# Cutting every 24th matmul of the w_out product into two column parts

## The chip, the cores and the metric

The kernel runs on one core of one Trainium2 chip. The metric is device time of one execution in microseconds (us); lower is better. Three runs of the kernel before took 463.36, 464.67 and 464.75 us, so its median is 464.67 us.

## The reference

The program is a chain of three layers with no normalisation between them, all in float32:

```python
# q, k, v: (2, 12, 448, 64)
scores = q @ k.T / sqrt(64), masked above the diagonal
x = softmax(scores) @ v                      # 2 x 448 tokens, 768 wide
g = relu(x @ w_in) ** 2                      # w_in (768, 2048)
y = g @ w_out                                # w_out (2048, 768): the product that is changed
h = max(y @ w1, y @ w2, y @ w3)              # w1..w3 (768, 768)
out = h @ w_o                                # (768, 768)
```

## The kernel before

Activations lie transposed, features on the 128 partitions and tokens along the columns, so that a block of 128 x 128 weights is the stationary operand of a matmul and the 448 tokens of one batch entry are its moving operand. A matmul of this kind is one instruction that loads the weights and one that streams the 448 columns into a bank of PSUM.

The dense layers are computed in a split form. Every value is cut into a high part that the float32r format holds and a remainder (`hi_lo`, L119), and a product is three passes (`PASSES`, L477): high by high, high by low, low by high. All matmuls of the dense layers are float32r; scores, transposes and the product with v are plain float32.

The products with w_in and with w1 to w3 (`Sevens.run`, L496) use seven block products in place of eight, as Strassen's scheme has it. They run from L499, 448 columns each, nine matmuls to a slot. The last product (`product`, L749, and the loop at L1009) has 384 columns to a matmul.

The w_out product is plain. It is made by `out_slots` (L610), which is called for the six blocks m of 128 output features. For each, the 16 blocks f of the inner dimension come in slots of two or three f; for each f, the three passes; for each pass, the two batch entries b, which share their weights and have a bank of PSUM each. That is 6 x 16 x 3 x 2 = 576 matmuls, all from L627. A slot's weights (`Quarter`, L181) are made by one cast on ScalarE and one subtraction on VectorE three slots ahead. At the end of a block m, ScalarE copies the two banks out (L644).

The order of the work is written out by hand. The attention's steps follow the list `ORDER`; after them the loop at L997 goes through the slots, issues the slot's matmuls, and then what stands `beside` it on the other engines. The first two blocks of the w_out product are interleaved with the last two slots of the w_in product. The matmuls of TensorE run in the order in which they are issued.

Of the kernel before, what the change touches and what calls it, by code (L numbers as in the profile page):

```python
# [18 lines left out]
MASKED = -1.0e30  # L19
WARM = 10  # L20
PR = 2
NORM = ((4, 7), (2, 4), (0, 2))
LEAD = 3
RING = 5
# [40 lines left out]
def tile_attention_moe_moe(  # L65
# [23 lines left out]
    nc = tc.nc  # L89
    B, NP, P, S = k.shape  # L90
# [8 lines left out]
    KFF = DFF // P  # L99
# [95 lines left out]
    def decoded(w):  # L195
        return Op(w.join, [Op(w.cast)], w)
# [98 lines left out]
    def constants(pool):  # L295
        ident = shared["ident"] = pool.tile([P, P], F32, name="ident", bufs=1)
        make_identity(nc, ident)
        for m, parts in ((NQ * P, 1), (S, 2)):
            n = P // parts
            mask = pool.tile([P, m], F32, name=f"mask{parts}", bufs=1)  # L300
            nc.gpsimd.memset(mask, 0.0)
            for j in range(parts):
                r = slice(j * n, (j + 1) * n)
                nc.gpsimd.affine_select(
                    out=mask[r, m - n:], in_=mask[r, m - n:], compare_op=ALU.is_ge, fill=MASKED,
                    base=0, pattern=[[-1, n]], channel_multiplier=1,
                )
            masks.append(mask)
# [5 lines left out]
    start = [kc * S - kc * (kc - 1) // 2 * P for kc in range(NK)] + [S * NK - NK * (NK - 1) // 2 * P]  # L314
# [6 lines left out]
    class Pair:  # L321
# [30 lines left out]
        def least(self, u):  # L352
            if not hasattr(self, "st"):
                self.pr = prs[self.i % PR]
                self.st = att.tile([P, 3, 2 * NQ + 1], F32, tag="st", name="st")
# [92 lines left out]
        def steps(self):  # L448
# [4 lines left out]
            for c in range(len(keys)):  # L453
# [5 lines left out]
                e[f"n{c}'"] = lambda c=c: self.norm(nc.vector, c)  # L459
            for n, c in enumerate(NORM):  # L460
                e[f"r{n}"] = lambda c=c: self.recip(*c)
# [145 lines left out]
    ]  # L607
    gh, gl, y = {}, {}, {}

    def out_slots(m):  # L610

        acc = [ps[i][:, :S] for i in ((6, 7), (0, 1), (2, 3), (4, 5), (6, 7), (0, 1))[m]]
        res = []
        for k0 in range(0, KFF, KDM):
            nk = min(KDM, KFF - k0)
            w = Weight(w_out, k0, nk, m * P, P, 2)
            d, h = decoded(w), -(-nk // 2)
            for r0, r1 in ((0, h), (h, nk)):
                quarter = Quarter(
                    [d], lambda w=w, r0=r0, r1=r1: w.t[:, r0:r1], lambda w=w: w.kept, r1 - r0  # L620
                )

                def run(quarter=quarter, k0=k0 + r0, k1=k0 + r1):
                    for f in range(k0, k1):
                        for e, (ew, ex) in enumerate(PASSES):
                            for b in range(B):
                                nc.tensor.matmul(  # L627
                                    acc[b], quarter.t[:, ew, f - k0], (gh, gl)[ex][f][0][:, b],
                                    start=f == 0 and e == 0, stop=f == KFF - 1 and e == 2,
                                    skip_group_check=True,  # L630
                                )
                    if m == KDM - 1:
                        for f in range(k0, k1):
                            units.give(gh[f][1])
                            units.give(gl[f][1])

                res.append(Slot(run, quarter, None, (m, k0 + r0)))

        def evac():
            if m == KDM - 1:  # L640
                shared["y"] = acc
                return [], []
            y[m] = units.take(f"y{m}", F32)
            return [lambda b=b: nc.scalar.copy(y[m][0][:, b], acc[b]) for b in range(B)], []  # L644

        res[-1].evac = evac
        return res
# [8 lines left out]
    ]  # L656
    head, tail = pipelined(firsts)
    outs = [out_slots(m) for m in range(KDM)]
    slots = head + [outs[0][0], tail[0], outs[0][1], tail[1], *outs[0][2:]]
    for e in outs[1:]:  # L660
# [157 lines left out]
    at = dict(load=0)  # L818
# [137 lines left out]
    with tc.tile_pool(name="att", bufs=2) as att:  # L956
        constants(att)
        prs = [att.tile([P, offs[-1]], F32, name=f"pr{n}", bufs=1) for n in range(PR)]
        warm = att.tile([P, 2 * P], FR, name="warm", bufs=1)
# [11 lines left out]
        for n in range(BESIDE):  # L971
            x, nm = slots[n].name
# [36 lines left out]
    for f in range(KF2):  # L1009
        x = zr["t"][0][:, f] if f < KH else None  # L1010
        x = [x[:, 0], x[:, 1]] if f < KH else [e[0][:, last] for e in z2[f]]
        for e, (ex, ew) in enumerate(((0, 0), (0, 1), (1, 0))):
            for acc, cs in zip(rest, (left, right)):
                nc.tensor.matmul(  # L1014
                    acc, x[ex], wo[f][ew][0][:, cs], start=f == 0 and e == 0,
                    stop=f == KF2 - 1 and e == 2, skip_group_check=True,
# [110 lines left out]
```

## Time and profile before

| | before |
|---|---|
| median of three runs | 464.67 us |
| profiled execution, its own time | 468.29 us |
| its span, first to last instruction | 466.5 us |
| outside the span | 1.8 us |
| granted TensorE clock, mean | 1.000 |
| matmuls and weight loads | 2434 each |
| matmuls of L627 | 576 |

Rows come from one profiled execution, whose time is 3.6 us above the median of the runs without a profile. PE is TensorE streaming columns, PEld TensorE loading weights; the two overlap. DVE is VectorE, ACT ScalarE, POOL GpSimd. Matmuls are pipelined, and the duration that a row gives for one of them is modelled and longer than its distance to the next, so distances are read from the chain of waits, which lists merged stretches with their start, their length and the count of instructions.

### The profile page before, as it was taken

What the parts mean: (1) busy time and instruction counts of PE and PEld (TensorE: products, weight loads), DVE (VectorE), ACT (ScalarE), POOL (GpSimd) and SP (SyncE); (2) the same over time, 40 slices, a digit from 0 to 9 for tenths busy, and PEclk for the clock granted to TensorE, in tenths of its full rate; (3) what the DMA queues carried; (4) which work ended last, traced back from release to release, by engine and by line L of the source; (5) the groups of instructions that cost most, each with busy time, mean ns of one, the idle gap of its engine ahead of it and who ended that gap; (6) DMA issues with size and microseconds to landing.
All of it is one profiled execution on the core that took longest, in us unless ns stands there. A gap on an engine that the chain in (4) does not pass through costs nothing.

```text
span 466.5 us, 6969 instructions
## 1 busy us (share of the span) xinstructions
PE 460.7 (99%) x2434; PEld 402.0 (86%) x2434; DVE 364.3 (78%) x813; ACT 283.1 (61%) x609; POOL 42.4 (9%) x90
## 2 busy tenths in 40 slices
PE   8999999999999999999999999999999999999997
PEld 5766676899999999899999999999999999999996
DVE  5999999998888899992322272898888988898963
ACT  5999999756555557952323254566457656665541
POOL 3656455000000000000000000000000000000000
PEclk9999999999999999999999999999999999999999
DMA  6463543223344441435323423342256466400014
GB/s 214 138 219 127 173 161 91 69 73 112 96 127 136 137 135 45 136 108 186 98 84 112 136 74 111 131 135 68 91 182 197 147 199 203 136 1 1 34 52 152
DMA packets 47619, 56.28 MB, mean 121 GB/s; under 512 B 1761, under 2 KB 43873, under 8 KB 47585
## 3 DMA queue, kind: packets, MB, share of 16 engines
q1 hardware_dynamic: 47296, 55.61, 37.0%
q8 instruction: 19, 0.31, 0.3%
q10 hardware_dynamic: 288, 0.23, 0.2%
q14 instruction: 16, 0.12, 0.1%
HBM read 53.08 MB, written 2.75 MB: 120 GB/s over the span
## 4 chain that ended last, share of the span: by engine, by line
PE 96%; DVE 3%; issue 0%; DVEq 0%
PE ps L499 47%; PE ps L627 26%; PE ps L752 7%; PE ps L347 7%; PE ps L386 4%; PE ps L417 4%; PE ps L1014 1%; PE ps L962 1%; DVE pr L358 1%; DVE s L124 0%; DVE pr L378 0%; DVE a L117 0%; DVE wd L169 0%; DVE st L374 0%; DVE wq L117 0%
## 5 line engine op out<-in xcount | busy, mean ns | idle before, releaser
L499 PE MATMUL ps<-s,wq 128*128 128x448 f32 x612 | 129.6, 368 | 0.0
L499 PEld LDWEIGHTS ps<-s,wq 128*128 128x128 f32 x612 | 114.8, 188 | 11.7 <-ACT s L509 0.2
L499 PE MATMUL ps<-a,wq 128*128 128x448 f32 x459 | 100.0, 370 | 0.0
L627 PE MATMUL ps<-gh,wq 128*128 128x448 f32 x384 | 95.3, 368 | 0.0
L499 PEld LDWEIGHTS ps<-a,wq 128*128 128x128 f32 x459 | 85.5, 188 | 9.0 <-issue 0.4
L117 DVE TENSOR_TENSOR wq<-wd,wq 128x384 fp32r<-128x384 f32 (+1 forms) x87 | 46.0, 533 | 49.3 <-ACT wq L114 45.0
L627 PEld LDWEIGHTS ps<-gh,wq 128*128 128x128 f32 x384 | 72.1, 188 | 7.3
L114 ACT CAST wq<-wd 128x384 fp32r<-128x384 f32 (+1 forms) x87 | 42.9, 499 | 53.8 <-PE ps L627 33.1
L164 ACT CAST up<-wr 128x768 f16<-128x768 bf16 (+1 forms) x58 | 60.8, 1049 | 7.1 <-DMA wr<-in_moe_w 2.1
L169 DVE SCALAR_TENSOR_TENSOR wd<-wr,up 128x768 int32<-128x768 int32 (+1 forms) x58 | 53.8, 928 | 6.1 <-ACT up L164 5.4
L627 PE MATMUL ps<-gl,wq 128*128 128x448 f32 x192 | 55.2, 368 | 0.0
L509 ACT COPY s<-ps 128x448 f32<-128x448 f32 x51 | 27.1, 533 | 37.6 <-PE ps L499 37.1
L366 ACT ACTIVATE pr<-pr,st 128x384 f32<-128x384 f32 (+3 forms) x84 | 44.1, 529 | 5.4 <-DVE st L358 5.2
L117 DVE TENSOR_TENSOR wq<-wt,wq 128x384 fp32r<-128x384 f32 x68 | 37.2, 551 | 9.4 <-ACT wq L114 9.1
L114 ACT CAST wq<-wt 128x384 fp32r<-128x384 f32 x68 | 34.3, 515 | 16.5 <-DVE wt L124 13.4
L378 POOL TENSOR_SCALAR pr<-pr,st 128x256 f32<-128x256 f32 (+3 forms) x77 | 39.9, 534 | 37.6 <-DVE st L374 22.7
L627 PEld LDWEIGHTS ps<-gl,wq 128*128 128x128 f32 x192 | 36.0, 188 | 3.6
L358 DVE CUSTOM_DVE_ANT_0 pr<-ps,mask 128x384 f32<-128x384 f32 (+3 forms) x84 | 34.5, 443 | 5.5 <-PE ps L347 4.9
L347 PE MATMUL ps<-k,q 64*128 64x128 f32 (+3 forms) x168 | 35.5, 445 | 0.0
L386 PEld LDWEIGHTS ps<-ident,pr 128*128 128x128 f32 x192 | 21.6, 140 | 7.5 <-issue 3.1
L386 PE MATMUL ps<-ident,pr 128*128 128x128 f32 x192 | 26.3, 276 | 0.3 <-DVE pr L378 0.3
L124 DVE TENSOR_TENSOR s<-ps,s 128x448 f32<-128x448 f32 (+1 forms) x31 | 18.2, 598 | 9.4 <-ACT s L509 4.5
(108 smaller groups left out, 494.0 us busy)
## 6 DMA issues: line engine op xcount, KB each, us to landing
wr<-in_moe_w_out SPq DMA_DIRECT2D x18, 768.0 KB, 4.3
wr<-in_moe_w SPq DMA_DIRECT2D x18, 768.0 KB, 4.3
wr<-in_moe_w_in SPq DMA_DIRECT2D x16, 768.0 KB, 4.7
v<-in_v SPq DMA_DIRECT2D x12, 256.0 KB, 4.6
wr<-in_moe_w_out SPq DMA_DIRECT2D x6, 512.0 KB, 3.5
q<-in_q SPq DMA_DIRECT2D x11, 256.0 KB, 2.7
out<-s SPq DMA_DIRECT2D x14, 192.0 KB, 1.9
k<-in_k SPq DMA_DIRECT2D x11, 224.0 KB, 2.9
```

What stands on the lines that cost most here:

```text
L114: nc.scalar.copy(hi, src)
L117: nc.vector.tensor_tensor(out=lo, in0=src, in1=hi.bitcast(F32), op=SUB)
L164: nc.scalar.copy(self.up.bitcast(FH)[:, :, 1::2], self.top)
L169: nc.vector.scalar_tensor_tensor(out=self.t.bitcast(I32), in0=self.rest, scalar=13, in1=self.up.bitcast(I32), op0=ALU.logical_shift_right, ...
L347: nc.tensor.matmul(sc[:, :keys[w]], self.n["q"][r, w // 2 * P:(w // 2 + 1) * P], self.n["k"][r, :keys[w]], start=True, stop=True,)
L358: nc.vector.tensor_tensor_reduce(out=self.pr[:, offs[u]:offs[u] + n], in0=self.sc[u][:, :n], in1=mask[:, mask.shape[1] - n:], scale=-SCALE ...
L366: nc.scalar.activation(sl, sl, ACTF.Exp, bias=self.st[:, 0, u:u + 1], scale=-1.0, accum_out=self.st[:, 1, u:u + 1],)
L378: engine.tensor_scalar(sl, sl, self.st[:, 2, u:u + 1], 1.0, op0=ALU.mult, op1=ALU.mult)
L386: nc.tensor.transpose(pt[:, i], self.pr[:, offs[u] + kc * P:offs[u] + (kc + 1) * P], shared["ident"])
L499: nc.tensor.matmul(self.acc[n], self.q[n].t[:, ew, i], X[OPERANDS[n]][i][:, ex], start=n in ("M1", "M2", "M5") and i == 0 and e == 0, stop ...
L627: nc.tensor.matmul(acc[b], quarter.t[:, ew, f - k0], (gh, gl)[ex][f][0][:, b], start=f == 0 and e == 0, stop=f == KFF - 1 and e == 2, skip ...
L752: nc.tensor.matmul(acc, a, b, start=start and i == 0 and e == 0, stop=i == KH - 1 and e == 2, skip_group_check=True,)
```

## The change

`matmul_in_parts` takes the place of the call at L627. It counts its calls; where the count leaves a remainder of 12 when divided by 24, it issues two matmuls with the same weights in place of one, the first over columns 0 to c and the second over columns c to 448 of the same bank. The cut c goes through a list of twelve places, so that each is used twice. The 576 calls give 24 such pairs: in each block m at f = 2, 6, 10 and 14, pass high by high, b = 0. No flag of these matmuls starts or ends an accumulation.

```diff
+EVERY = 24
+CUTS = (224, 256, 288, 320, 352, 384, 400, 416, 432, 440, 192, 128)
...
+    nth = [0]
+
+    def matmul_in_parts(acc, w, x, start, stop):
+
+        n, at = nth[0], [0, S]
+        nth[0] += 1
+        if n % EVERY == EVERY // 2:
+            at.insert(1, CUTS[n // EVERY % len(CUTS)])
+        for c0, c1 in zip(at, at[1:]):
+            nc.tensor.matmul(
+                acc[:, c0:c1], w, x[:, c0:c1], start=start, stop=stop, skip_group_check=True,
+            )
+
...
                             for b in range(B):
-                                nc.tensor.matmul(
+                                matmul_in_parts(
                                     acc[b], quarter.t[:, ew, f - k0], (gh, gl)[ex][f][0][:, b],
-                                    start=f == 0 and e == 0, stop=f == KFF - 1 and e == 2,
-                                    skip_group_check=True,
+                                    f == 0 and e == 0, f == KFF - 1 and e == 2,
                                 )
```

## Rows read from the trace of the kernel before

**Rows 1.** The page: span, busy time by engine, granted clock, chain by engine and line.
```profile
span 466.5 us, 6969 instructions
PE 460.7 (99%) x2434; PEld 402.0 (86%) x2434; DVE 364.3 (78%) x813; ACT 283.1 (61%) x609; POOL 42.4 (9%) x90
...
PEclk9999999999999999999999999999999999999999
...
PE 96%; DVE 3%; issue 0%; DVEq 0%
PE ps L499 47%; PE ps L627 26%; PE ps L752 7%; PE ps L347 7%; PE ps L386 4%; PE ps L417 4%; PE ps L1014 1%; PE ps L962 1%; DVE pr L358 1%; DVE s L124 0%; DVE pr L378 0%; DVE a L117 0%; DVE wd L169 0%; DVE st L374 0%; DVE wq L117 0%
```

**Rows 2.** Chain in order of time (start, us, what, count), the w_out stretch.
```profile
183.81 3.65 PE ps L627 x18
187.46 2.03 PE ps L499 x9
189.49 3.72 PE ps L627 x18
193.21 1.86 PE ps L499 x9
195.07 111.60 PE ps L627 x540
```

**Rows 3.** Chain in order of time, from the w_out stretch to the end.
```profile
306.67 113.46 PE ps L499 x549
...
428.53 6.24 PE ps L1014 x36
434.77 28.30 PE ps L752 x162
463.07 0.02 issue
463.09 0.56 DVE s L124
```

**Rows 4.** Waits of the weight loads from 187 us to the end.
```profile
PEld ps L499 <- ACT s L509: 0.3, 1, 0.3
PEld ps L752 <- issue: 0.2, 1, 0.2
```

**Rows 5.** Instructions in order of time, weight loads alone, after a pause of float32r work.
```profile
88.66 0.19 PEld L499 LDWEIGHTS ps<-a,wq 128*128 128x128 f32 x1
...
88.76 0.40 PEld L499 LDWEIGHTS ps<-a,wq 128*128 128x128 f32 x2
```

**Rows 6.** The same around the restart at 444 us.
```profile
444.06 0.19 PEld L752 LDWEIGHTS ps<-piece 128*128 128x128 f32 x1 [0.25 <-issue]
...
444.17 0.19 PEld L752 LDWEIGHTS ps<-piece 128*128 128x128 f32 x1
```

**Rows 7.** Chain in order of time, attention: transposes and plain float32 scores.
```profile
24.33 0.87 PE ps L386 x8
...
30.73 0.76 PE ps L347 x2
```

**Rows 8.** Groups by shape, matmuls: columns of the moving operand, count, busy us, mean ns.
```profile
L347 PE MATMUL ps<-k,q 128*128 128x448 f32 x24 | 10.9, 545 | 0.0
...
L962 PE MATMUL ps<-warm 128*128 128x256 f32 x10 | 2.5, 432 | 2.0 <-DVE warm L960 2.0
```

**Rows 9.** Groups by shape, weight loads of the w_out product.
```profile
L627 PEld LDWEIGHTS ps<-gh,wq 128*128 128x128 f32 x384 | 72.1, 188 | 7.3
...
L627 PEld LDWEIGHTS ps<-gl,wq 128*128 128x128 f32 x192 | 36.0, 188 | 3.6
```

**Rows 10.** Waits on the w_out matmuls, 183 to 307 us (total us, times, longest).
```profile
ACT wq L114 <- PE ps L627: 33.1, 13, 3.3
ACT y L644 <- PE ps L627: 14.2, 4, 3.6
```

## The prediction

> **What bounds the kernel now.** First the page. TensorE streams columns for 460.7 of 466.5 us, no other engine is above 78%, and the chain that ended last lies 96% on TensorE, 26% of the span on L627, the line that is changed [rows 1]. The granted clock stands at its full value, the 2.4 GHz level, in every slice, so the clock is not what is at stake.
>
> Next the chain in order of time, which gives the distance from one matmul to the next. In the w_out stretch one piece holds 540 matmuls of L627 in 111.60 us: 206.7 ns each, with nothing between them [rows 2]. So the stretch has no idle time into which an added instruction could go. The waits say the same from the other side: ScalarE waits 33.1 us and 14.2 us for these matmuls [rows 10], and TensorE waits for nobody there.
>
> Then what comes behind. From 306.67 us 549 matmuls of L499 take 113.46 us, again 206.7 ns each, and the last product runs to 463.07 us [rows 3]. The waits of the weight loads from 187 us on add up to 0.5 us in two places [rows 4]. A delay of TensorE in the w_out product is therefore not swallowed later, beyond at most that 0.5 us: the other engines only get more time to be ready. Nothing of the order on the other engines changes, no wait is added, and no buffer comes free earlier.
>
> The time of the change is thus the time that 24 pairs take on TensorE, less that of 24 whole matmuls, and nearly all of it shows at the end.
>
> **What a pair costs.** Each of the 24 removed matmuls gives back 206.7 ns [rows 2]. Each pair adds one instruction of weight loading, since in this kernel every matmul has a load of its own, also the two of b = 0 and b = 1 that share weights (2434 of each [rows 1]).
>
> The wide part first. The trace has float32r matmuls of two widths at full clock: 448 columns at 206.7 ns, and 384 columns at 6.24 us / 36 = 173.3 ns [rows 3]. That is 33.4 ns for 64 columns, 0.52 ns per column. I take this line for all wide parts: 440 columns 202.5 ns, 416 190, 400 181.7, 352 156.6, 320 139.9, 288 123.2, 256 106.5. With 0.417 ns per column (one column per cycle at 2.4 GHz) from the 384-column point down, 320 columns would be 146.6 and 256 120 ns.
>
> The narrow part next. The trace shows no float32r matmul at full clock under 384 columns, so its cost has to be bounded. From below: the weights of the matmul behind it have to be loaded while it streams. Where float32r work sets in after a pause, two loads start one right behind the other, at 88.66 and 88.76 us and again at 444.06 and 444.17 us [rows 5, 6]; at the rows' precision that is 0.10 to 0.11 us, and I take 108 ns. Transposes of 128 columns with one load each follow each other at 0.87 us / 8 = 109 ns [rows 7]. So a matmul cannot follow the last sooner than 108 ns, however narrow, unless the load is hidden by something else. In the stretch as it is, the 206.7 ns of the columns hide it; with a narrow part that cover is gone, and the load is what is late next. From above: the load's own recorded duration is 188 ns [rows 9], and the shortest distance seen between float32r matmuls without a pause is the 173.3 ns of 384 columns; if that already were the load's limit, every narrow part would cost 173.3 ns. (The ten matmuls of 256 columns at the program's start take 0.25 us each [rows 8], longer than those of 384 and 448 columns later. What holds them is peculiar to the start, so they set no end; with parts at 0.25 us the sum would be 24 x 293 ns = 7.0 us.) I take 108, because the two restarts show float32r loads at that distance themselves and no row shows a load that held up a matmul for longer.
>
> The sum, each pair as the larger of line and 108 ns for either part, less 206.7 ns, in the order of the cuts: 224, 256 and 192: 9.3 ns each (two times 108); 288: 24.5; 320 and 128: 41.2 each; 352: 57.9; 384: 74.6; 400: 82.9; 416: 91.3; 432: 99.7; 440: 103.8. Together 645 ns, and each cut comes twice: **1.29 us**. The line is not critical: with 0.417 ns per column under 448 instead, the sum is 1.36 us. With a floor of 110 ns it is 1.35 us. With a fixed 13.3 ns for every part on top of the load (a floor of 121) it is 1.70 us.
>
> Against the profiled execution: 468.29 + 1.3 = 469.6 us, with a span of 467.8. Against the median of the runs: 464.67 + 1.3 = **466.0 us**, 0.28% more.
>
> **What speaks against it.** The row shows 206.7 ns for 448 columns [rows 2]. The Trainium skill ("TensorE: Matmul & The Clock Gate", section "Back-to-back issue gap") gives an isolated distance of N / 2.4 + 2.5 ns, and names a floor by the count of columns only; by it, as an estimate, 448 columns would take 189.2 ns and a pair 191.7 ns, so that the change would cost 24 x 2.5 ns = 0.06 us, not to be measured. The trace doesn't agree at 448 columns: it is 17.5 ns slower, and the rule leaves the weight load out. Its result lies beside that of the third rival.
>
> **The rivals.**
>
> *Short float32r matmuls stream at the plain float32 pace.* Plain float32 scores of 448 columns run as two instructions each of 0.76 us / 2 = 0.38 us [rows 7] (x24 for twelve such matmuls [rows 8]), so 0.76 us for 448 columns, 1.70 ns per column. If a float32r matmul under some width fell back to that, and 256 is the narrowest float32r width in the kernel [rows 8], then the parts of 224 columns would take 380 ns each, 192 326, 160 271, 128 217, 96 163, and the parts of 64 columns and fewer would stay at the load's 108. The sum is then 553 + 2 x 227 + 188 + 2 x 150 + 113 + 75 + 83 + 91 + 100 + 104 = 2061 ns, twice: 4.1 us, 468.8 us. For it: no row shows a short float32r matmul at the fast pace. Against it: the fast pace comes with the operand's type, and the program names the same type for all parts. Chance 0.17.
>
> *The load behind a narrow part takes 173 ns, not 108.* The sum is 7 x 140 + 140 + 148 + 157 + 165 + 169 = 1759 ns, twice: 3.5 us, 468.2 us. For it: the recorded 188 ns, and that loads follow each other at 173.3 ns even in the 384-column stretch, whose columns alone would take 160 ns. Against it: the restarts at 0.10 and 0.11 us. A partial form (a floor of 121 to 140 ns) gives 1.7 to 2.3 us. Chance 0.14.
>
> *Narrow parts escape the surcharge of a wide matmul, and no load shows (not slower).* 448 columns take 206.7 ns, where 448 columns at one a cycle take 186.7; the line above meets the one-a-cycle time at 256 columns, so a cut could save up to 20 ns if a part of up to 256 columns took its columns' time only. By the line for the wide parts and 0.417 ns per column for the narrow ones the 24 pairs would give back 0.26 us: 464.4 us. The point that decides is whether the second load of the same weights is hidden: below some 50 ns per load the narrow parts are free, at 108 they are not. For it: no row shows a second load of weights that are already in place behind a narrow part. Against it: the restarts and the transposes [rows 5 to 7]. Chance 0.08.
>
> That the change doesn't do what it says I hold for unlikely: the counter runs once through 576 calls, and 24 of them are cut. If the two parts became one instruction again, the time would be 464.7 us; chance 0.02.
>
> **How the numbers follow.** The forecast, 466.0 us, has the remaining 0.59; its own range is 465.2 to 466.8 us (sums of 0.9, the 1.29 less most of the later waits, to 1.7 us, and some 0.4 us of measurement). The range that holds 8 in 10 has to reach to the slower rivals, 468.2 and 468.8 us, and on the other side to just under the median: 464.6 to 468.8 us. About 0.3%, 1.4 us, is what a measurement of this kernel can tell from no change. The forecast's 1.3 us lies just under that bound, so its chance goes to both sides: 0.34 within, 0.25 slower. The two slower rivals give 0.29 of slower (a little of it, the partial form at its low end, may fall within). The third rival and the undone change lie within, with 0.04 left for faster. In all: faster 0.04, within 0.3% 0.43, slower 0.53.
>
> **What would show it.** In the profile after there are 2458 matmuls and as many loads. The chain's w_out stretch is longer by 1.3 us and everything behind it is shifted by as much, with L499 at 206.7 ns as before. Between a narrow part and the next matmul lie 108 ns whatever the narrow width; a distance of 370 to 380 ns at the cut of 224 shows the plain float32 pace, one of 173 ns at all narrow parts the second rival, distances under 60 ns at the parts of 8 to 64 columns the third. Wide parts on the line: 202 ns at 440, 140 at 320. The prediction is wrong if the weight load doesn't set the floor, if the pace depends on width below 256 columns, or if a stall elsewhere moves by more than the pairs cost.

## The result and the profile after

The changed kernel took 468.14 us (four runs, 467.96 to 468.49), the kernel before beside it 464.45 us (four runs, 463.36 to 464.75): a ratio of 1.0085, interval 1.0067 to 1.0103, or 3.7 us. The intervals here and below cover the runs of one group (one chip, one time), and the ratios are of all runs, not of the medians. The forecast was 466.0 us with a range of 464.6 to 468.8. The sign and the range hold; the size is 3.7 us where 1.3 were forecast, and 468.14 lies outside the forecast's own narrower range of 465.2 to 466.8.

The profile of the changed kernel does not show these 3.7 us. First the page: span and busy times (the rows of before are [rows 1]).

```profile
span 466.5 us, 7017 instructions
## 1 busy us (share of the span) xinstructions
PE 460.8 (99%) x2458; PEld 404.1 (87%) x2458; DVE 364.2 (78%) x813; ACT 283.2 (61%) x609; POOL 42.6 (9%) x90
```

The 24 added matmuls and loads are there, yet the span is the same 466.5 us. The chain of waits in order of time (start, us, what, count) says the same for the stretches of [rows 2, 3]; L621 is what L627 was, L501 what L499 was.

```profile
194.79 111.89 PE ps L621 x563
306.67 113.46 PE ps L501 x549
```

563 matmuls, 23 pairs among them, take 111.89 us where 540 took 111.60. The matmuls behind take 113.46 us as before. So the pairs seem to cost 0.3 us in the traces and 3.7 us in the times. Two things explain both.

**The pairs cost what was forecast.** The starts of the weight loads around the second pair of 224 and 224 columns:

```profile
249.34 0.19 PEld L621 LDWEIGHTS ps<-gh,wq 128*128 128x128 f32 x1
249.44 0.19 PEld L621 LDWEIGHTS ps<-gh,wq 128*128 128x128 f32 x1
249.55 0.19 PEld L621 LDWEIGHTS ps<-gl,wq 128*128 128x128 f32 x1
249.76 0.19 PEld L621 LDWEIGHTS ps<-gl,wq 128*128 128x128 f32 x1
```

And around the first pair of 440 and 8 columns:

```profile
234.36 0.19 PEld L621 LDWEIGHTS ps<-gh,wq 128*128 128x128 f32 x1
234.56 0.19 PEld L621 LDWEIGHTS ps<-gh,wq 128*128 128x128 f32 x1
234.67 0.19 PEld L621 LDWEIGHTS ps<-gl,wq 128*128 128x128 f32 x1
234.88 0.19 PEld L621 LDWEIGHTS ps<-gl,wq 128*128 128x128 f32 x1
```

In this trace a load starts within 0.01 us of the matmul ahead of the one that it serves. The rows show 0.10 and 0.11 us for parts of 224 columns, and for the part of 8 columns (from 234.56) again 0.11 us, near the floor of 108 ns that was forecast. What speaks for the load, and not the matmul, as what is late is the record of the whole matmul behind the 8 columns:

```profile
234.59 0.46 PE L621 MATMUL ps<-gh,wq 128*128 128x448 f32 x1
```

It begins 0.03 us after its own load (234.56, recorded at 0.19 us), while that load still runs, and the next load starts only at 234.67. From the first to the last of these loads are 0.42 and 0.52 us, where two whole matmuls take 0.413: the pairs cost some 0.01 and 0.11 us (forecast 9 and 104 ns). The wide parts are on the forecast line at 440 columns (0.20 us) but not at 320, where the loads lie 0.15 us apart and 0.140 were forecast:

```profile
264.18 0.19 PEld L621 LDWEIGHTS ps<-gh,wq 128*128 128x128 f32 x1
```
```profile
264.33 0.19 PEld L621 LDWEIGHTS ps<-gh,wq 128*128 128x128 f32 x1
```

**The whole matmuls around them have two rhythms.** Two stretches of the chain in the changed kernel, the first behind the pair cut at 320, the second behind the pair cut at 352:

```profile
205.14 4.26 PE ps L621 x21
```
```profile
210.07 4.13 PE ps L621 x20
```

That is 202.9 and 206.5 ns a matmul, the short and the long rhythm. The trace of before has 206.7 in its whole stretch of 540, but both rhythms stand in [rows 2]: the first 18 matmuls of L627 take 3.65 us, 202.8 ns each, the next 18 take 3.72 us, 206.7 each. Between them, at 187 us, lies the wait of 0.3 us for ScalarE [rows 4]. A pair doesn't only cost its time, it also leaves the matmuls behind it in one rhythm or the other. In this trace the stretches behind 288, 352, 432, 192 and 128 columns (both times each) and behind the second 256 are long, the others short. The pairs' cost in the trace is thus mostly given back by matmuls at 202.7 ns. Why the times still differ by 3.7 us is what the experiments had to show: the trace of before was an execution with the long rhythm from 188 us on, and the runs of before, by their times, were mostly not.

### The profile page after: what moved, and what is told of

Its sections match the earlier page's. It is cut to its first block, busy times and chain, and to the rows that moved or that the text cites. A ratio compares the mean times of both kernels' runs of the same rounds, so it can differ in the third digit from the quotient of the medians.

```text
span 466.5 us, 7017 instructions
## 1 busy us (share of the span) xinstructions
PE 460.8 (99%) x2458; PEld 404.1 (87%) x2458; DVE 364.2 (78%) x813; ACT 283.2 (61%) x609; POOL 42.6 (9%) x90
## 4 chain that ended last, share of the span: by engine, by line
PE 96%; DVE 3%; issue 0%; DVEq 0%
PE ps L501 47%; PE ps L621 26%; PE ps L766 7%; PE ps L349 7%; PE ps L388 4%; PE ps L419 4%; PE ps L1028 1%; PE ps L976 1%; DVE pr L360 1%; DVE s L126 0%; DVE pr L380 0%; DVE a L119 0%; DVE wd L171 0%; DVE st L376 0%; DVE wq L119 0%
## 5 line engine op out<-in xcount | busy, mean ns | idle before, releaser
L501 PE MATMUL ps<-s,wq 128*128 128x448 f32 x612 | 129.5, 368 | 0.0
L501 PEld LDWEIGHTS ps<-s,wq 128*128 128x128 f32 x612 | 114.8, 188 | 11.6 <-ACT s L511 0.2
L501 PE MATMUL ps<-a,wq 128*128 128x448 f32 x459 | 99.9, 370 | 0.0
L621 PE MATMUL ps<-gh,wq 128*128 128x448 f32 (+7 forms) x408 | 96.0, 358 | 0.0
L501 PEld LDWEIGHTS ps<-a,wq 128*128 128x128 f32 x459 | 85.6, 188 | 8.9 <-issue 0.4
L621 PEld LDWEIGHTS ps<-gh,wq 128*128 128x128 f32 x408 | 75.8, 188 | 6.4
L621 PE MATMUL ps<-gl,wq 128*128 128x448 f32 x192 | 54.8, 366 | 0.0
L621 PEld LDWEIGHTS ps<-gl,wq 128*128 128x128 f32 x192 | 36.1, 188 | 2.7
```

Source lines behind the costliest of these rows:

```text
L501: nc.tensor.matmul(self.acc[n], self.q[n].t[:, ew, i], X[OPERANDS[n]][i][:, ex], start=n in ("M1", "M2", "M5") and i == 0 and e == 0, stop ...
L621: nc.tensor.matmul(acc[:, c0:c1], w, x[:, c0:c1], start=start, stop=stop, skip_group_check=True,)
```

## The experiments

Two theories stood against each other. R: the rhythm, and what sets it, makes most of the difference. C: the pairs cost the 3.7 us wherever they stand. Kernels of one group ran on one chip and share the runs of before.

**The kernel before, again.**

> The kernel before, unchanged, timed against itself. Theory R (two rhythms): the 448-column matmuls can follow each other at 206.7 or at 202.7 ns; the profile of before had 206.7 throughout and 468.3 us, the timed runs of before 464.5 us, so the timed runs had the quicker rhythm in some 900 of its 1650 such matmuls (900 x 4 ns = 3.6 us). It expects that this profile shows 202.7 ns in one of its long stretches whenever its own time is near 464, and 206.7 everywhere when it is near 468. Theory P (the profiler or the chip makes the 3.6 us, nothing in the program): every profile of before reads 468 with 206.7 ns, every timed run 464. Ratio 1.000 by both.

It took 465.42 us (12 runs, 463.36 to 468.95), the shared runs of before 467.85 (35 runs, 463.99 to 469.06): ratio 0.9987, interval 0.9955 to 1.0018. The same program is spread over 5 us. The profiled execution took 465.13 us, with a span of 463.3; in every run, profiled or not, the span is 1.7 to 1.9 us below the time, and a profiled execution can be near 465 us too. So the profile does not make the 3.6 us, and P falls. Its chain:

```profile
195.29 109.44 PE ps L627 x540
304.73 112.20 PE ps L499 x549
```

540 matmuls take 109.44 us, 202.7 ns each, 2.16 us less than in the first trace of before. The records of the matmuls from 200 to 300 us (shortest, median and longest duration, ns) differ too, the first trace of before above, this one below:

```profile
L627 PE MATMUL ps<-gh,wq x324: 368/368/369, 199.7 to 299.9; 128*128 128x448 f32 x162
```
```profile
L627 PE MATMUL ps<-gh,wq x331: 362/365/369, 199.8 to 299.9; 128*128 128x448 f32 x166
```

In the long rhythm all are alike, and the loads start 206 or 207 ns apart. In the short one the distances of the loads run through a cycle of five, about 198, 207, 203, 203 and 202 ns. The stretch behind has both rhythms; the chain before and after 376 us:

```profile
305.94 69.13 PE ps L499 x341
```
```profile
376.84 37.19 PE ps L499 x180
```

202.7 and 206.6 ns. Between them TensorE waits once, for ScalarE's copy out of the bank that it needs (waits of the weight loads, 375.3 to 376.6 us):

```profile
PEld ps L499 <- ACT s L509: 0.2, 1, 0.2
```

R holds in these two executions: the one at 465.13 us has the short rhythm from the w_out product to 376 us, the one at 468.29 the long one. Before the w_out product they do not differ: in both, and in every kept trace without a pair in the w_in product, the long rhythm runs from 90 to 180 us. In all the traces a change of rhythm stands at a pair or where one load starts late, by 0.06 us or more, mostly for a wait for ScalarE, as at 187 us in the first trace and at 376 us here; not every such delay changes it.

**The same cuts, another order.**

```diff
-CUTS = (224, 256, 288, 320, 352, 384, 400, 416, 432, 440, 192, 128)
+CUTS = (224, 256, 288, 320, 352, 128, 400, 416, 432, 440, 192, 384)
```

> The changed kernel with the same twelve cuts in another order: 384 and 128 change places, so that the last pair before the products with w1 to w3 is 384 and 64 columns, after which the changed kernel's trace shows 202.7 ns, in place of 128 and 320, after which it shows 206.7. The work is the same. Theory R: the 549 matmuls behind run at 202.7 ns, 549 x 4.0 = 2.2 us less than in the changed kernel: some 466.0 us. Theory C (the pairs themselves cost the 3.7 us, wherever they stand): 468.1 us, and 206.7 ns behind the last pair.

466.61 us (12 runs, 465.82 to 467.05), beside the same runs of before: ratio 0.9987, interval 0.9965 to 1.0009. So with 24 pairs the kernel is no slower than before was in this group; the changed kernel did not run in it. The work is that of the changed kernel; its chain has

```profile
195.45 111.95 PE ps L621 x563
307.41 111.26 PE ps L501 x549
```

111.26 us behind the w_out product where the changed kernel has 113.46: the 2.2 us of R. The time is 0.6 us above the 466.0 of R and 1.5 below the 468.1 of C. C falls.

**One pair, the last, cut at 384.**

```diff
-        if n % EVERY == EVERY // 2:
-            at.insert(1, CUTS[n // EVERY % len(CUTS)])
+        if n == 564:
+            at.insert(1, 384)
```

> One pair in place of 24, the last of them (call 564), cut at 384 columns. Theory R: +0.08 us for the pair, and the 549 matmuls behind it at 202.7 ns; up to there as in the kernel before, so between 2.1 us faster than before (where before ran at 206.7 ns behind the pair) and the same (where it ran at 202.7). Theory C: a twenty-fourth of 3.7 us, +0.15 us, 206.7 ns behind the pair as in the profile of before.

465.85 us (464.11 to 467.82), ratio 0.9984, interval 0.9957 to 1.0011. Its trace has the long rhythm up to the pair and the short one behind it, until some 378 us:

```profile
306.83 32.22 PE ps L501 x159
```
```profile
379.82 35.34 PE ps L501 x171
```

That is 202.6 and 206.7 ns. As R has it, but the rhythm that a single pair sets holds only until a wait changes it: not the one near 351 us, but the one near 378. Its gain lies within the spread.

**One pair early in the w_in product.** The cut is in `Sevens.run`, at the 48th matmul of that line, 384 columns.

```diff
+                    if nth[0] == FIRST_CUT:
+                        at.insert(1, 384)
```

> No pair in the w_out product; one matmul of the w_in product early in it (the 48th of its line, at some 90 us) is cut at 384 columns. Theory R: the rhythm behind it is 202.7 ns, and if nothing sets it back some 1600 matmuls gain 4.0 ns each: up to 6.4 us less span than the profile of before, near 462 us; if the joint of the w_in and w_out products sets it back, 460 of them gain, 1.8 us. Theory C: +0.08 us, no other change.

463.43 us (462.07 to 467.42) against 467.85, ratio 0.9938, interval 0.9909 to 0.9968. One added matmul makes the kernel faster, and its quickest run is below every run of before (463.31). Its chain behind the pair:

```profile
91.84 88.27 PE ps L508 x436
```

202.5 ns each, where the second trace of before has there

```profile
91.97 88.04 PE ps L499 x426
```

206.7 ns. It kept the short rhythm until about 348 us.

**The changed kernel, again.**

> The changed kernel, unchanged, in more runs beside more runs of before. Theory R: before is spread over 463.4 to 469.1 us, as its rhythm behind the w_in product falls out one way or the other, and the four runs of before that stood beside the prediction were of the quick kind; the changed kernel stays within half a microsecond of 468.1, since its last pairs set the rhythm to 206.7 ns each time. So a ratio within 0.4% of 1, not 1.0085. Theory C (the change itself costs 3.7 us): the ratio stays near 1.008.

468.73 us (9 runs, 467.95 to 468.95) against 464.53 us of before (32 runs, 463.31 to 468.71): ratio 1.0070, interval 1.0042 to 1.0099. The narrow spread of the changed kernel, 1.0 us, came as R has it, up to 0.85 us above the 468.1 where half a microsecond was expected. The expected ratio missed: I took the 35 runs of the first group for the rule, where 8 of 35 runs of before were under 466 us, but in this group 20 of 32 were. How often before falls into the short rhythm differs from group to group (a third had 13 of 23), and with it the measured ratio.

**All pairs at 128.**

```diff
+CUTS = (128,)
```

> All 24 pairs cut at 128 (128 and 320 columns), after which the traces so far show 206.7 ns. Theory R: the w_out product and the products behind it run at 206.7 ns in every run; the pair costs 41 to 47 ns (its distances in the changed kernel: 460 ns for three matmuls' starts in place of 413), 24 x 47 = 1.1 us on an execution of before that has the slow rhythm throughout (468.3): 469.4 us, with little spread. Theory C: 24 pairs at the mean price of the changed kernel's, 3.7 us over 464.5: 468.2.

465.27 us (464.59 to 469.68), ratio 1.0032, interval 0.9997 to 1.0067. Missed: the runs fall into two lots, eight at 464.6 to 465.8 and four at 468.7 to 469.7. The trace, of an execution at 464.62 us, has the short rhythm in both stretches:

```profile
194.44 110.72 PE ps L621 x563
305.16 111.27 PE ps L501 x549
```

So a cut at 128 doesn't set the long rhythm, it leaves the rhythm that it meets. In the changed kernel it met the long one, set by the cut at 192 ahead of it. The upper lot is, by its time, the 469.4 us that was expected for the long rhythm; no trace of it was kept. The pairs here cost (110.72 - 109.44) / 23 = 56 ns, where 41 were forecast, or 45 with the removed matmul counted at 202.7; the 320-column part is the 10 ns slower that the changed kernel's trace shows.

**All pairs at 224.**

```diff
+CUTS = (224,)
```

> All 24 pairs cut at 224, after which the traces so far show 202.7 ns. Theory R: pairs at 10 ns, 0.25 us; 1100 matmuls from the w_out product on gain 4.0 ns each, 4.4 us, on the 468.3 of the slow rhythm: 464.1 us, up to 1.5 us later where a wait behind the last pair sets the rhythm back. So 5 us between this kernel and that with 128, of which the pairs themselves make 0.9. Theory C: the pairs alone, 0.9 us between the two kernels.

464.41 us (12 runs, 463.54 to 465.24), ratio 0.9972, interval 0.9946 to 0.9998. The chain:

```profile
196.16 109.66 PE ps L621 x563
305.82 111.26 PE ps L501 x549
```

Short rhythm in both, and 23 pairs for 109.66 - 109.44 = 0.22 us, 10 ns each. The 5 us against the kernel with 128 holds for its upper lot only.

**The changed kernel with one pair more, cut at 224, behind the last.**

```diff
+        if n == 570:
+            at.insert(1, 224)
```

> The changed kernel with one pair more: call 570, the sixth from the last of the w_out product, is cut at 224 too, so 25 pairs. Theory R: 0.01 us for the pair, and 549 matmuls behind it at 202.7 in place of 206.7 ns: 2.2 us less than the changed kernel, some 466.3 us, less of that where a wait sets it back. Theory C: 0.01 to 0.1 us more than the changed kernel, 468.5.

466.34 us (12 runs, 465.79 to 466.87), ratio 1.0008 to before, interval 0.9981 to 1.0035. It ran in another group than the changed kernel, and is 1.8 and 2.4 us below that kernel's two medians, with more work. The chain:

```profile
195.48 111.88 PE ps L623 x564
307.36 111.26 PE ps L501 x549
```

The w_out product is as in the changed kernel (111.89), the products behind are 2.20 us shorter. This is the plainest test: one added matmul takes away that part of the loss.

**One pair alone, cut at 192.**

```diff
+        if n == 564:
+            at.insert(1, 192)
```

> One pair alone, call 564, cut at 192 (192 and 256 columns), behind which the traces show 206.7 ns from either rhythm. Theory R: the 549 matmuls behind run at 206.7 ns in each run, so no run comes near the quick runs of before (463.4): the quickest 463.4 + 549 x 4.0 ns = 465.6 us, the slowest 468.3, where the w_out product too has the slow rhythm. Theory C: a single pair costs about 0.01 us, the spread stays 463.4 to 469.

466.22 us (464.75 to 468.03), ratio 1.0005, interval 0.9979 to 1.0032. The three quickest of twelve runs are below the bound of 465.6. The trace is that of the quickest, 464.75 us; its chain behind the pair and later:

```profile
305.00 43.19 PE ps L501 x209
```
```profile
351.87 62.26 PE ps L501 x307
```

206.7 ns, and from some 350 us on 202.8: again a wait for ScalarE, of 0.3 us, lies between, and this time it changed the rhythm to the short one. The pair did what was expected of it; that nothing changes it back was wrong.

**A pair of 224 in every 48 of all 448-column matmuls.** The kernel takes `matmul_in_parts` into the products with w_in and w1 to w3 too.

```diff
+EVERY = 48
+CUT = 224
...
+        if nth[0] >= EVERY and not start and not stop:
+            at.insert(1, CUT)
+            nth[0] = 0
```

> A pair of 224 and 224 columns at about every 48th of all 448-column float32r matmuls (w_in, w_out, w1 to w3), never one that starts or ends an accumulation. Theory R: 202.7 ns almost throughout, some 1600 x 4.0 = 6.4 us off 468.3, plus 34 pairs x 10 ns = 0.35 us: some 462.3 us with a spread under 1 us. Theory C: each pair costs, so slower than before.

462.77 us (12 runs, 462.38 to 463.51) against 464.53, ratio 0.9945, interval 0.9921 to 0.9968; the changed kernel took 468.73 in the same group. This kernel beats both, with a spread of 1.1 us where before has 5. Its chain in the w_in product has 443 matmuls, the pairs among them, in the time of 426 of before:

```profile
91.99 88.12 PE ps L492 x443
```

## Why the prediction was right and where it was not

*Right: the cost of a pair.* The floor of 108 ns behind a narrow part is what the loads show at 224 and at 8 columns. The line for the wide parts is right at 440 columns and some 10 ns too low at 320. The sum of 1.29 us can be set against the trace: 540 matmuls at 202.7 ns are 109.44 us, the stretch took 111.89, 2.45 more. Eleven of its stretches, ten of some 22 matmuls each and the last of 11, have the long rhythm, at 4.0 ns a matmul some 0.9 to 1.0 us. That leaves about 1.5 us for 23 pairs; forecast for these were 1.28, or 1.37 where the removed matmul is counted at 202.7. Of the sums beside the main one, that with 0.417 ns per column under 448 comes to 1.53 us, not 1.36. The 191.7 ns of a pair by the column rule count no floor for the narrowest parts, though the same sentence names one. And the ten matmuls at the start begin from 2.0 to 4.1 us, some 0.23 us apart and not 0.25; what holds them there no run shows. None of these changes the forecast.

*Right: the rivals' rejection.* Parts of 224 columns at 0.10 and 0.11 us exclude the plain float32 pace (380 ns) and the floor of 173 ns. The load's floor shows, so narrow parts are not free either. The measured 3.7 us lie between the sums of the two slower rivals (3.5 and 4.1 us), which is chance: neither happens. It is also luck that 468.14 lies in the range: its upper end, 468.8, was set by these rivals. And "slower" holds against runs of before that were mostly quick; a kernel with as many pairs, in another order, was level with before in its group.

*Wrong: "464.67 + 1.3".* The sum was worked out in the 206.7 ns rhythm of the profiled execution and added to a median whose runs had the other. The 3.6 us between 468.29 and 464.67 stood in the text and no cause was asked for, though [rows 2] have matmuls of L627 at 202.8 ns beside those at 206.7. Most of the 3.6 us is the rhythm: every run's span follows its time at 1.7 to 1.9 us, and an execution of before at 465.13 us shows 202.7 ns from the w_out product to 376 us.

*Wrong: "everything behind it is shifted by as much, with L499 at 206.7 ns as before".* It is at 206.7 in the changed kernel, but in the runs of before, by their times, mostly not. The prediction took the distance of whole matmuls for fixed; its last sign of being wrong was a stall elsewhere that moves by more than the pairs cost; what moved was no stall but that distance, by 1.3 to 2.2 us over the 549 matmuls behind. Against the second trace of before the difference has two parts:

| us | before, first trace | before, second trace | changed | changed, one pair more |
|---|---|---|---|---|
| 540 calls of the w_out product | 111.60 | 109.44 | 111.89 | 111.88 |
| 549 matmuls behind | 113.46 | 112.20 | 113.46 | 111.26 |

2.45 us in the product, of which some 1.5 are the pairs and 1.0 the long stretches, and 1.26 us behind it (2.20 where before keeps the short rhythm to the end). Together 3.7 us. That this is the measured 3.7 is in part chance: the second trace of before is an execution 0.7 us above the median, and it enters the w_out product 0.5 us later than the changed kernel's (195.29 and 194.79 us), so the two traces differ by 3.2 us. The cut at 192 leaves the long rhythm, the last cut at 128 keeps it, and with them the changed kernel goes into the products behind it at 206.7 ns. It is slow steadily, where before is slow in some executions and not in others.

*What is not settled.* The traces show that the rhythm exists, that it changes at cuts and at delays of 0.06 us or more, and what single cuts did: 384, 224 and 192 set one, 128 kept the one that it met, 256 left once the one and once the other. Why 448 columns take either 202.7 or 206.7 ns, and why before falls into the one more often in one group of runs than in another, no run here tells. The measured ratio is therefore one of frequencies: 1.0085 and 1.0070 in two groups; against the runs of the group where before was mostly long (467.85) the changed kernel's 468.1 to 468.7 us would be 0.1 to 0.2% more, but it didn't run in that group.

## What to carry to other kernels

When a profile's own time lies 0.8% above the median of the runs, ask which stretch differs before adding anything to either: here a second trace of the same program had another matmul distance in 900 of its matmuls. On a bound engine read the distance of its instructions, from the chain's length over its count, in every stretch and every trace, since a small change can alter it far behind the place that was edited. A comparison of a program that is spread over 5 us needs more than four runs, and more than one group: 35 runs of before had a median of 467.85 us and 32 in another group 464.53, so not even tens of runs of one group settle it. An edit that only steadies the program can be worth more than its own cost.

## What the runs showed of the hardware

Float32r matmuls of 448 columns, each with its own load, follow each other at 206.7 or at 202.7 ns with a granted clock of 1.00 in both (2.4 GHz level). Added instructions can make a bound stream faster: one 224-column pair costs 10 ns and set the 549 matmuls behind it 4.0 ns quicker each. The long rhythm is one distance, the short one a cycle of five, and in these traces it changes only at a cut or where a load comes late. Float32r matmuls with a weight load each came no closer than some 0.11 us, at 8 columns as at 224; the records at 8 columns speak for the load as what was late, and no run has such matmuls without a load each.
